# The last 3072 tokens' first product as Strassen's seven block products, in windowed attention with a gated feed-forward on one core

## The chip, the cores and the metric

One core of a Trainium2 chip runs one program. The metric is the device time of a run in microseconds (us). TensorE (PE) multiplies matrices into eight accumulation banks (PSUM); DVE, ACT and POOL are the vector, scalar and general engines; SP only issues DMAs. Each engine executes its own queue in order.

## The reference

```
q, k, v: 8 batches x 8 heads x 576 positions x 64, float32
scores = q @ k.T / sqrt(64); heads 0-3 see the last 32 positions,
         heads 4-7 every fourth position of the last 128
attn   = softmax(scores); x = attn @ v, as 4608 tokens x 512
h = x @ w_in                     # 512 x 2048, the first product
g = h * clip(h + 3, 0, 6) / 6
out = g @ w_out                  # 2048 x 512, the second product
```

## The kernel before

**Precision.** A float32 operand of a large product is split into a high and a low part (`xh`, `xl` for tokens, two rows of `wt[f]` for each weight, `gh`, `gl` for the gated values), and a product is three matmuls: high by high, high by low, low by high.

**Work units.** Tokens come in 12 chunks of 384 (`CH`), the 2048 hidden features in 16 blocks `f` of 128 (`NF`). A step is one pair (chunk, `f`): `gemm1` makes 128 features x 384 tokens with 4 x 3 matmuls of 384 columns into one of the two banks of `ps_h`; `relu`, `gate`, `gate_high`, `gate_low` turn it into `gh` and `gl` on ACT and DVE; two steps later (`LAG`) `gemm2` multiplies three tiles of 128 tokens by the rows of `w_out`, 3 x 3 matmuls of 512 columns, into three banks of `ps_a` that collect over the 16 values of `f`, and at the last one ACT scales them into a tile `o` and stores it.

**Attention.** It is cut into 48 trios of 12 blocks of 32 queries (`trios`, in `_order`). `st_both(ts, tv)` puts the scores of one trio and the values of another on TensorE in one block of 48 small matmuls (`block`), with two banks of `ps_a`; then `normalise` divides the values, `largest` and `shifted` prepare the exponent, `exponent` runs on ACT. `turn_by_blocks` transposes by DVE plus four DMAs on SP's queue. `st_split` writes the finished tokens into `xh` (ACT, `high`) and `xl` (POOL, `low`). `xh` and `xl` hold three chunks at a time.

**Order.** The first 12 trios, the loading and conversion of the weights and the steps of the first two chunks stand in a hand-written order (`ORDER`) that fixes ACT, DVE and SP. After it (`step_at`) TensorE's order is that of the program text, and the other engines' queues are ordered by a planner: among operations that its own estimate of durations has as ready, the one with the lowest `turn_of` value goes first. The remaining trios are placed at half steps by the list `at`, first every 6 halves (3 steps), from the eleventh on every 8. Values of a trio run in the block after its scores.

**SBUF.** Weights, staging tiles, the first trios' loads and `o` share a pool `wpool` of 18 slots of 8 KB a partition.

Of the kernel before, what the change touches and what calls it, by code (L numbers as in the profile page):

```python
# [23 lines left out]
SPARE = 2  # L24
WORK = 12
# [3 lines left out]
NLOAD = 3  # L29
# [4 lines left out]
NEG = -1.0e30  # L34

# [24 lines left out]
h25 Q27 l25 H16 RE26 GL9 w26@H17 k12 k13 k14 v12 v13 v14 M2 RE19 T26 T19 G21 GH26 GH19 Q26 H9 U26 s26 U27 j26 H7  # L60
# [5 lines left out]
def windowed_attention_ffn(ctx: ExitStack, tc: tile.TileContext, qk, vp, w, mask, out):  # L66
# [44 lines left out]
    wpool = ctx.enter_context(tc.tile_pool(name="wpool", bufs=NF + SPARE))  # L111
# [40 lines left out]
    wide = {}  # L152

    def load_tile(t, name, at, n):

        if t >= NWIDE:
            return loads.tile([P, n], F32, name=name, tag=name)
        if t not in wide:
            wide[t] = wpool.tile([P, 4, DM], F32, name="first", tag="w").rearrange("p a n -> p (a n)")
        return wide[t][:, at : at + n]  # L160

    def load_qk(t):
        if t < T and t not in kqs:
            kqs[t] = load_tile(t, "kq", 0, KW + CH)
            ins = nc.sync.dma_start(out=kqs[t], in_=qk[t].rearrange("h d x -> (h d) x"))
            in_turn(ins)
            return ins

    def load_v(t):
        if t < T and t not in vs:  # L170
            v = load_tile(t, "v", KW + CH, TB * W)
            vs[t] = v.rearrange("p (n x) -> p n x", x=W)
            return nc.sync.dma_start(out=v, in_=vp[t].rearrange("h k x -> (h k) x"))
# [67 lines left out]
    def normalise(t):  # L241
        pv = pvs.pop(t)[:, : SLOTS * W].rearrange("p (s x) -> p s x", x=W)
        z = small.tile([P, SLOTS], F32, name="z")
        nc.vector.tensor_scalar_add(z, pv[:, :, D], 1e-9)
# [10 lines left out]
        wide.pop(t, None)  # L255
        if t >= NFIRST:
            load_v(t + NLOAD)
        return ins
# [4 lines left out]
    def block(ts, tv):  # L263

        ps = ps_a.tile([P, 512], F32, name="ps_a") if ts is not None else None
        pv = ps_a.tile([P, 512], F32, name="ps_a") if tv is not None else None
# [17 lines left out]
    def st_both(ts, tv):  # L284
        block(ts, tv)
        if tv is not None:
            normalise(tv)
        if ts is not None:
            largest(ts)
            shifted(ts)  # L290
            exponent(ts)
# [42 lines left out]

    def pieces_of(t):

        b, kind, part = trios[t]
        xu = xfs[t].rearrange("p (u f) -> p u f", u=2)
        half = CH // 2
        to = lambda x: x[:, 2 * kind : 2 * kind + 2, b % 2 * S : b % 2 * S + S]  # L340
        if kind == 0:
            return [(xu, lambda x: to(x)[:, :, half * part : half * (part + 1)])]
        found, at = [], half * part
        while at < half * (part + 1):
            c, i0 = divmod(at, CLS)
            n = min(CLS - i0, half * (part + 1) - at)
            found.append((
                xu[:, :, at - half * part : at - half * part + n],
                lambda x, c=c, i0=i0, n=n: to(x).rearrange("p u (i c) -> p u c i", c=DIL)[:, :, c, i0 : i0 + n],
            ))  # L350
            at += n
        return found

    def high(t):
        b, kind, part = trios[t]
        assert all(read[c] == NF for c in chunks(b - 2, kind, part))
        for src, view in pieces_of(t):
            ins = nc.scalar.copy(view(xh), src)  # L358
        return ins

    def low(t, eng):
        for src, view in pieces_of(t):
            ins = eng.tensor_tensor(out=view(xl), in0=src, in1=view(xh).bitcast(F32), op=ALU.subtract)  # L363
# [4 lines left out]
    def st_split(t):  # L368
        high(t)
        low(t, nc.gpsimd)  # L370
# [9 lines left out]
    steps += [(c, f) for c in range(2, NCH) for f in range(NF)]  # L380
# [6 lines left out]
    wt, staged, converted = {}, {}, set()  # L387
    WN = w.shape[3]

    def load_w(p):  # L390
        st = wpool.tile([P, 4, WN], F32, name="st", tag="w")
        ins = nc.sync.dma_start(
            out=st[:, 0:2].rearrange("p a n -> p (a n)").bitcast(U32), in_=w[p // 2, p % 2].bitcast(U32)
        )
        in_turn(ins)
        staged[p] = st
        return ins

    def parts(p):
        st = staged[p]  # L400
        words = st[:, 0:2].rearrange("p a n -> p (a n)").rearrange("p (n w) -> p n w", w=2)
        return words[:, :, 1], words[:, :, 0], st[:, 2], st[:, 3]

    def cv_product(p):
        if p // 2 not in wt:
            wt[p // 2] = wpool.tile([P, 4, WN], F32R, name="wt", tag="w")
# [24 lines left out]
    def cv_high(p):  # L431
        ins = nc.scalar.copy(wt[p // 2][:, p % 2 * 2], parts(p)[2])
# [3 lines left out]
    def cv_low(p):  # L436
        hi, lo = (wt[p // 2][:, p % 2 * 2 + i] for i in range(2))
# [5 lines left out]

    phs, ts, ghs, gls, po, done = {}, {}, {}, {}, {}, set()
# [4 lines left out]
    def gemm1(n):  # L449
# [5 lines left out]
        for kt in range(NK):  # L455
            a, b = xh[:, kt, r0 : r0 + CH], xl[:, kt, r0 : r0 + CH]
            ks = slice(kt * P, (kt + 1) * P)
            nc.tensor.matmul(ph, lhsT=wt[f][:, 0, ks], rhs=a, start=(kt == 0), stop=False)  # L458
            nc.tensor.matmul(ph, lhsT=wt[f][:, 0, ks], rhs=b, start=False, stop=False)  # L459
            ins = nc.tensor.matmul(ph, lhsT=wt[f][:, 1, ks], rhs=a, start=False, stop=(kt == NK - 1))  # L460
        phs[n] = ph
        return ins
# [15 lines left out]

    def gemm2(n):
        c, f = steps[n]  # L480
        assert 2 * f + 1 in converted
        gh, gl = ghs.pop(n), gls.pop(n)
        first = c not in po
        if first:
            po[c] = [ps_a.tile([P, DM], F32, name="ps_o", tag="ps_a") for _ in range(TT)]
        if f == NF - 1:
            o = wpool.tile([P, TT, DM], F32, name="o", tag="w")
        for tt in range(TT):
            rows = slice(tt * P, (tt + 1) * P)
            nc.tensor.matmul(po[c][tt], lhsT=gh[:, rows], rhs=wt[f][:, 2], start=first, stop=False)  # L490
            nc.tensor.matmul(po[c][tt], lhsT=gh[:, rows], rhs=wt[f][:, 3], start=False, stop=False)  # L491
            ins = nc.tensor.matmul(po[c][tt], lhsT=gl[:, rows], rhs=wt[f][:, 2], start=False, stop=(f == NF - 1))  # L492
            if f == NF - 1:
                if n < len(steps) - 1 or tt < TT - 1:
                    nc.scalar.mul(o[:, tt], po[c][tt], 1.0 / 6.0)
                else:
                    half = DM // 2
                    nc.scalar.mul(o[:, tt, :half], po[c][tt][:, :half], 1.0 / 6.0)
                    nc.vector.tensor_scalar_mul(o[:, tt, half:], po[c][tt][:, half:], 1.0 / 6.0)
                r = c * CH + tt * P  # L500
                nc.scalar.dma_start(out=out[r : r + P, :], in_=o[:, tt])
        done.add(n)
        return ins

# [40 lines left out]
    halves = [(c, f, k) for c in range(2, NCH) for f in range(NF) for k in range(2)]  # L545
# [3 lines left out]
    place(-3, lambda: st_both(NFIRST, None))  # L549
    place(-3, lambda: ats.update({NFIRST: turn_by_blocks(es.pop(NFIRST), "a")}))  # L550
    for i, p in enumerate(at):
        t = NFIRST + i
        more = t + 1 < T
        place(p, lambda t=t, more=more: st_both(t + 1 if more else None, t))
        place(p, lambda t=t: xfs.update({t: turn_by_blocks(xs.pop(t), "xf")}))
        if more:
            place(p, lambda t=t: ats.update({t + 1: turn_by_blocks(es.pop(t + 1), "a")}))
        place(p + 4, lambda t=t: st_split(t))
# [37 lines left out]
    while n < len(steps) + LAG:  # L596
        step_at(n)
        n += 1

# [93 lines left out]
```

## Time and profile before

| | |
|---|---|
| median of 3 runs | 897.35 us (895.88 to 897.6) |
| profiled execution, span | 896.5 us |
| profiled execution, its own time beside the span | not listed; the median run is 0.85 us over the span |
| PE busy | 879.8 us, 98% |
| DVE, ACT, POOL busy | 450.2, 339.4, 43.7 us |
| mean TensorE clock granted | 0.997 |
| moved by DMA | 74.87 MB, mean 84 GB/s |

A row of a group of instructions gives line, engine, operation, tile written <- tiles read, shapes and count, then the busy total in us and the mean of one in ns, then the idle time of the engine just before and what ended it. A row of the timeline gives start, duration, engine and line; in brackets the idle time before it and what ended that. A row of the windows gives the stretch, its length, the busy time of the engines, the granted clock, the DMA share and GB/s. `L458` is a line of the listing above; DMA issues stand under their queue (SPq, ACTq). TensorE's printed durations are pipelined; distances between starts are what one costs.

### The profile page before, as it was taken

The page shows a single profiled execution, that of the slowest core. Times are in us where ns is not written, and L with a number is a line of the kernel's source. Part 1 is how long each engine was busy: PE and PEld are TensorE (multiplying, and loading weights), DVE is VectorE, ACT ScalarE, POOL GpSimd, SP SyncE. Part 2 cuts the span into 40 slices and gives each one's busy share as a digit, 9 for nine tenths or more (in the row PEclk, how much of TensorE's full clock was granted, in tenths as well). Part 3 has the DMA queues.
Part 4 walks back from the last instruction along what each step waited for, and adds up shares of the span by engine and source line. Part 5 has one row for each costly group of instructions (what it writes and reads, how often), then busy time and mean ns, then how long its engine had stood idle before and what let it go on. Part 6 is the DMA issues. An engine that isn't in the chain of part 4 may idle for free.

```text
span 896.5 us, 20572 instructions
## 1 busy us (share of the span) xinstructions
PE 879.8 (98%) x8732; PEld 787.5 (88%) x8732; DVE 450.2 (50%) x952; ACT 339.4 (38%) x661; POOL 43.7 (5%) x60
## 2 busy tenths in 40 slices
PE   7799999999999999999999999999999999999998
PEld 4688898889898899989998999899989998899997
DVE  3899997355545454445444544554454445322222
ACT  3688775333332333223323333233223332422322
POOL 0000000001010100000100010001000100000000
PEclk9999999999999999999999999999999999999999
DMA  8756436132323122113112212222122110100000
GB/s 276 271 152 204 122 114 201 56 95 84 89 87 87 53 88 88 47 48 123 52 47 86 85 51 82 56 81 85 47 64 99 60 28 11 49 1 1 36 1 35
DMA packets 37804, 74.87 MB, mean 84 GB/s; under 512 B 7377, under 2 KB 16593, under 8 KB 37713
## 3 DMA queue, kind: packets, MB, share of 16 engines
q1 hardware_dynamic: 32528, 64.13, 23.3%
q10 hardware_dynamic: 5184, 9.44, 2.8%
q8 instruction: 68, 1.11, 0.5%
q14 instruction: 24, 0.19, 0.1%
HBM read 57.02 MB, written 9.44 MB: 74 GB/s over the span
## 4 chain that ended last, share of the span: by engine, by line
PE 96%; DVE 1%; DMA 1%; ACT 0%; issue 0%; SPq 0%
PE ps_h L458 16%; PE ps_h L459 15%; PE ps_h L460 15%; PE ps_o L490 15%; PE ps_o L492 15%; PE ps_o L491 15%; PE ps_a L211 3%; PE ps_a L193 2%; PE ps_a L296 1%; PE ps_a L203 1%; DMA first<-in_qk 1%; DMA mi<-in_mask 0%; DVE x L247 0%; PE ps_a L270 0%; DVE e L230 0%
## 5 line engine op out<-in xcount | busy, mean ns | idle before, releaser
L458 PE MATMUL ps_h<-xh,wt 128*128 128x384 f32 x768 | 264.0, 344 | 0.0
L460 PE MATMUL ps_h<-xh,wt 128*128 128x384 f32 x768 | 258.6, 337 | 0.0
L459 PE MATMUL ps_h<-xl,wt 128*128 128x384 f32 x768 | 258.6, 337 | 0.0
L469 DVE SCALAR_TENSOR_TENSOR t<-t,ps_h 128x384 f32<-128x384 f32 x192 | 105.0, 547 | 247.9 <-ACT t L466 246.5
L490 PE MATMUL ps_o<-wt,gh 128*128 128x512 f32 x576 | 224.5, 390 | 0.0
L491 PE MATMUL ps_o<-wt,gh 128*128 128x512 f32 x576 | 224.1, 389 | 0.0
L492 PE MATMUL ps_o<-wt,gl 128*128 128x512 f32 x576 | 224.0, 389 | 0.0
L466 ACT ACTIVATE t<-ps_h,three 128x384 f32<-128x384 f32 x192 | 110.7, 577 | 215.7 <-PE ps_h L460 210.4
L477 DVE TENSOR_TENSOR gl<-t,gh 128x384 fp32r<-128x384 f32 x192 | 107.1, 558 | 103.8 <-ACT gh L473 101.4
L458 PEld LDWEIGHTS ps_h<-xh,wt 128*128 128x128 f32 x768 | 144.8, 189 | 8.9
L459 PEld LDWEIGHTS ps_h<-xl,wt 128*128 128x128 f32 x768 | 144.7, 188 | 5.3
L460 PEld LDWEIGHTS ps_h<-xh,wt 128*128 128x128 f32 x768 | 144.6, 188 | 0.0
L473 ACT CAST gh<-t 128x384 fp32r<-128x384 f32 x192 | 98.4, 513 | 110.9 <-DVE t L469 97.3
L492 PEld LDWEIGHTS ps_o<-wt,gl 128*128 128x128 f32 x576 | 108.1, 188 | 22.8
L490 PEld LDWEIGHTS ps_o<-wt,gh 128*128 128x128 f32 x576 | 108.2, 188 | 15.5
L491 PEld LDWEIGHTS ps_o<-wt,gh 128*128 128x128 f32 x576 | 108.2, 188 | 15.5
L363 POOL TENSOR_TENSOR xl<-xf,xh 128x384 fp32r<-128x384 f32 (+3 forms) x54 | 43.1, 808 | 734.9 <-ACT xh L358 734.5
L239 ACT ACTIVATE e<-e 128x384 f32<-128x384 f32 x48 | 25.0, 524 | 139.9 <-DVE e L230 139.8
L211 PEld LDWEIGHTS ps_a<-v,a 64*32 64x32 f32 x1728 | 35.6, 105 | 12.7 <-issue 12.7
L193 PE MATMUL ps_a<-kq 64*32 64x64 f32 x1872 | 45.7, 225 | 0.0
L358 ACT CAST xh<-xf 128x384 fp32r<-128x384 f32 (+3 forms) x72 | 33.6, 532 | 22.7 <-DMA xf<-xf_t 22.6
L211 PE MATMUL ps_a<-v,a 64*32 64x65 f32 x1728 | 41.4, 225 | 0.0
(48 smaller groups left out, 489.3 us busy)
## 6 DMA issues: line engine op xcount, KB each, us to landing
st<-in_w SPq DMA_DIRECT2D x32, 512.0 KB, 4.2
kq<-in_qk SPq DMA_DIRECT2D x39, 416.0 KB, 4.5
v<-in_v SPq DMA_DIRECT2D x39, 390.0 KB, 3.6
out<-o ACTq DMA_DIRECT2D x36, 256.0 KB, 2.3
first<-in_qk SPq DMA_DIRECT2D x9, 416.0 KB, 5.1
first<-in_v SPq DMA_DIRECT2D x9, 390.0 KB, 4.8
a<-a_t SPq DMA_DIRECT2D x144, 24.0 KB, 1.8
xf<-xf_t SPq DMA_DIRECT2D x144, 24.0 KB, 2.5
```

The lines of the kernel that those rows point to most:

```text
L193: return nc.tensor.matmul(ps[at : at + QB, 2 * QB * i : 2 * QB * (i + 1)], lhsT=x[rows, KW + QB * n : KW + QB * (n + 1)], rhs=x[rows, QB * ...
L211: return nc.tensor.matmul(ps[at : at + QB, i * W : (i + 1) * W], lhsT=ats[t][rows, QB * n : QB * (n + 1)], rhs=vs[t][rows, n, :], start=Tr ...
L458: nc.tensor.matmul(ph, lhsT=wt[f][:, 0, ks], rhs=a, start=(kt == 0), stop=False)
L459: nc.tensor.matmul(ph, lhsT=wt[f][:, 0, ks], rhs=b, start=False, stop=False)
L460: ins = nc.tensor.matmul(ph, lhsT=wt[f][:, 1, ks], rhs=a, start=False, stop=(kt == NK - 1))
L466: return nc.scalar.activation(ts[n], phs[n], AF.Relu, bias=three, scale=1.0)
L469: return nc.vector.scalar_tensor_tensor(out=ts[n], in0=ts[n], scalar=6.0, in1=phs.pop(n), op0=ALU.min, op1=ALU.mult)
L473: return nc.scalar.copy(ghs[n], ts[n])
L477: return nc.vector.tensor_tensor(out=gls[n], in0=ts.pop(n), in1=ghs[n].bitcast(F32), op=ALU.subtract)
L490: nc.tensor.matmul(po[c][tt], lhsT=gh[:, rows], rhs=wt[f][:, 2], start=first, stop=False)
L491: nc.tensor.matmul(po[c][tt], lhsT=gh[:, rows], rhs=wt[f][:, 3], start=False, stop=False)
L492: ins = nc.tensor.matmul(po[c][tt], lhsT=gl[:, rows], rhs=wt[f][:, 2], start=False, stop=(f == NF - 1))
```

## The change

Chunks 0 to 3 stay as they were. Chunks 4 to 11 form four groups of two chunks, and the 16 blocks `f` eight pairs. For each group and pair, a 2 x 2 block matrix of tokens (two chunks by two halves of the 512 inputs) times a 2 x 2 block matrix of weights is formed with seven block products (Winograd's form of Strassen's scheme) where four steps of `gemm1` had eight. A block product is two inputs' tiles by three matmuls of 384 columns.

- **Weights.** `combine(k)`, placed at eight half steps of chunks 2 and 3, makes the four weight sums of pair `k` on POOL, splits them on ACT and DVE, and writes them and three plain blocks to a DRAM tile `sums` (11 DMAs on SP's queue). In every group `load_sums` streams `sums` back, 512 KB at a time, into tiles `ring`, eight ahead.
- **Tokens.** Finished tokens of chunks 4 on go by POOL copies into tiles `raw`; `add_tokens` makes four differences on POOL at the last pair of a group, and `fill_cell` splits each of the seven sources into `xh`, `xl` and a seventh pair of tiles after the last use of the old content.
- **A pair.** `pair` orders the seven products over two banks of `ps_h`: products accumulate in `x` and `y`, `kept` copies a bank on ACT, `added` adds a bank on DVE, `gated` is the chain to `gh` and `gl`. The second product's tiles wait in a list `units` and run between the products; a group's six output tiles hold all six banks of `ps_a`.
- **Attention.** Scores of trio t + 2 now share a block with the values of trio t. 17 blocks stand in chunks 2 and 3, about two steps apart; 21 stand in pairs, one in each of the first seven pairs of groups 0 to 2, and use the banks of `ps_h`, `largest` ahead of `normalise`.
- **Slots.** `wpool` has 36 slots of 4 KB; a trio's two loads, a stage and its conversion, and the two weights of an `f` have slots of their own. 16 work tiles (12 before), loads two ahead (three before).

```diff
-SPARE = 2
-WORK = 12
+SLOTS_W = 36
+WORK = 16
-NLOAD = 3
+NLOAD = 2
+PLAIN = 4
+RING = 8
+STEP_US = 4.1
...
+    def combine(k):
+        wa, wb = win[2 * k], win[2 * k + 1]
+        v = w_tile("v", [4, HALF])
+        for i, x in enumerate((wa, wb)):
+            ins = nc.gpsimd.tensor_tensor(
+                out=v[:, 2 * i : 2 * i + 2].rearrange("p a n -> p (a n)"), in0=x[:, 0].bitcast(F32), in1=x[:, 1].bitcast(F32), op=ALU.add
+            )
+            not_before(ins, last_gemm[0])
+        for to, a, b, op in ((3, 2, 3, ALU.add), (2, 0, 2, ALU.subtract), (0, 3, 0, ALU.subtract), (1, 1, 0, ALU.subtract)):
+            nc.gpsimd.tensor_tensor(out=v[:, to], in0=v[:, a], in1=v[:, b], op=op)
+        hi, lo = w_tile("sh", [4, HALF], F32R), w_tile("sl", [4, HALF], F32R)
+        split = nc.scalar.copy(hi, v)
+        nc.vector.tensor_tensor(out=lo, in0=v, in1=hi.bitcast(F32), op=ALU.subtract)
...
+    def load_sums(at):
+        if at < GROUPS * STREAM:
+            ring[at] = w_tile("ring", [2, 2, HALF], F32R)
+            ins = nc.sync.dma_start(out=ring[at].bitcast(F32), in_=sums[at % STREAM])
...
+    def add_tokens(g):
+        (b11, b12), (b21, b22) = ([raws.pop((2 * g + j, k)) for j in range(2)] for k in range(2))
+        t1, t2, t4 = (w_tile("t", [2, CH]) for _ in range(3))
+        minus = lambda to, a, b: nc.gpsimd.tensor_tensor(out=to, in0=a, in1=b, op=ALU.subtract)
+        minus(t1, b12, b11)
+        minus(t2, b22, t1)
+        minus(b12, b22, b12)
+        minus(t4, b21, t2)
+        sources[g] = {A11: b11, A12: b21, S2: t2, S1: t1, S3: b12, A22: t4, S4: b22}
+    def fill_cell(g, i):
+        src = sources[g].pop(i)
+        hi, lo = cell(i)
+        nc.scalar.copy(hi, src)
+        nc.vector.tensor_tensor(out=lo, in0=src, in1=hi.bitcast(F32), op=ALU.subtract)
...
+    def gated(h, g, f, j):
+        x = work_tile("t")
+        nc.scalar.activation(x, h, AF.Relu, bias=three, scale=1.0)
+        nc.vector.scalar_tensor_tensor(out=x, in0=x, scalar=6.0, in1=h, op0=ALU.min, op1=ALU.mult)
+        gh, gl = work_tile("gh", F32R), work_tile("gl", F32R)
+        nc.scalar.copy(gh, x)
+        nc.vector.tensor_tensor(out=gl, in0=x, in1=gh.bitcast(F32), op=ALU.subtract)
+        for tt in range(TT):
+            units.append(lambda tt=tt: unit_part(g, f, j, tt, gh, gl))
+    def multiply(g, k, i, bank, start):
+        at = PRODUCTS * k + i
+        tile_, (h, l) = ring[g * STREAM + at // 2][:, at % 2], cell(i)
+        for kt in range(2):
+            ks = slice(kt * P, (kt + 1) * P)
+            nc.tensor.matmul(bank, lhsT=tile_[:, 0, ks], rhs=h[:, kt], start=(start and kt == 0), stop=False, skip_group_check=True)
+            nc.tensor.matmul(bank, lhsT=tile_[:, 0, ks], rhs=l[:, kt], start=False, stop=False, skip_group_check=True)
+            nc.tensor.matmul(bank, lhsT=tile_[:, 1, ks], rhs=h[:, kt], start=False, stop=(kt == 1), skip_group_check=True)
+        if at % 2:
+            load_sums(g * STREAM + at // 2 + RING)
+        if k == NF // 2 - 1 and g + 1 < GROUPS:
+            fill_cell(g + 1, i)
...
+    def pair(g, k, n, beside):
+        fa, fb = 2 * k, 2 * k + 1
+        bank = lambda: ps_h.tile([P, CH], F32, name="ps_x", tag="ps_h")
+        soon = lambda us: turn_of(n + us / STEP_US)
+        soon(0)
+        x, y = bank(), bank()
+        multiply(g, k, A11, x, True)
+        soon(-8)
+        s = kept(x)
+        soon(1)
+        multiply(g, k, A12, y, True)
+        soon(-8)
+        h = added(s, y)
+        soon(-4)
+        gated(h, g, fa, 0)
+        soon(2)
+        run_units(1)
+        multiply(g, k, S2, x, False)
+        soon(-8)
+        s2 = kept(x)
+        y = bank()
+        soon(4)
+        multiply(g, k, S1, y, True)
+        run_units(2)
+        multiply(g, k, S3, x, False)
+        soon(-8)
+        s = kept(x)
+        h = added(s, y)
+        soon(-4)
+        gated(h, g, fb, 1)
+        soon(7)
+        run_units(3)
+        multiply(g, k, A22, x, False)
+        soon(-4)
+        gated(x, g, fb, 0)
+        soon(10)
+        multiply(g, k, S4, y, False)
+        soon(-8)
+        h = added(s2, y)
+        soon(-4)
+        gated(h, g, fa, 1)
+        soon(11)
+        run_units(3)
+        for step in beside:
+            step()
+        soon(14)
+        run_units(3)
...
-    at = [1, 7, 13, 19, 25, 31, 39, 45, 51, 57]
-    at += [at[-1] + 8 * (i + 1) for i in range(T - NFIRST - 10)]
+    BLOCKS = 16
+    for b in range(BLOCKS + 1):
+        p = round(1 + 4.07 * (b - 1))
+        take(b, lambda step: place(p, step), lambda step: place(min(p + 4, len(halves) - 1), step))
+    for b in range(BLOCKS + 1, T - NFIRST + 2):
+        g, k = divmod(b - BLOCKS - 1, 7)
+        put = lambda step: in_pair.setdefault((g, k), []).append(step)
+        take(b, put, put, ps_h)
+    for k in range(NF // 2):
+        place(4 + 6 * k, lambda k=k: combine(k))
```

More of the change, by code (lines that the diff above doesn't have):

```diff
@@ L289, in st_both @@
             largest(ts)
+        if pool is not None and tv is not None:
+            normalise(tv)
+        if ts is not None:
             shifted(ts)
@@ L477, in gate_low @@
         return nc.vector.tensor_tensor(out=gls[n], in0=ts.pop(n), in1=ghs[n].bitcast(F32), op=ALU.subtract)
-    def gemm2(n):
[L480 to L487, printed above, removed]
-        for tt in range(TT):
[L489 to L501, printed above, removed]
@@ new lines, in store, with out_tile @@
+    def store(o, bank, r, halves=False):
+        if not halves:
+            nc.scalar.mul(o, bank, 1.0 / 6.0)
+        else:
+            half = DM // 2
+            nc.scalar.mul(o[:, :half], bank[:, :half], 1.0 / 6.0)
+            nc.vector.tensor_scalar_mul(o[:, half:], bank[:, half:], 1.0 / 6.0)
+        nc.scalar.dma_start(out=out[r : r + P, :], in_=o)
+    outs = {}
+    def out_tile(c, tt):
+        if (c, tt // 2) not in outs:
+            outs[c, tt // 2] = w_tile("o", [2, DM])
+        return outs[c, tt // 2][:, tt % 2]
@@ new lines, in gemm2_part @@
+    def gemm2_part(n, tt):
+        c, f = steps[n]
+        gh, gl = ghs[n], gls[n]
+        first = f == 0
+        if first and tt == 0:
+            po[c] = [ps_a.tile([P, DM], F32, name="ps_o", tag="ps_a") for _ in range(TT)]
+        rows = slice(tt * P, (tt + 1) * P)
+        nc.tensor.matmul(po[c][tt], lhsT=gh[:, rows], rhs=wt(f, 2), start=first, stop=False)
+        nc.tensor.matmul(po[c][tt], lhsT=gh[:, rows], rhs=wt(f, 3), start=False, stop=False)
+        ins = nc.tensor.matmul(po[c][tt], lhsT=gl[:, rows], rhs=wt(f, 2), start=False, stop=(f == NF - 1))
+        if f == NF - 1:
+            store(out_tile(c, tt), po[c][tt], c * CH + tt * P)
+        return ins
@@ L502, in gemm2, with not_before @@
+    def gemm2(n):
+        assert 2 * steps[n][1] + 1 in converted
+        for tt in range(TT):
+            ins = gemm2_part(n, tt)
+        del ghs[n], gls[n]
         done.add(n)
         return ins
+    HALF = 2 * P
+    PRODUCTS = 7
+    A11, A12, S2, S1, S3, A22, S4 = range(PRODUCTS)
+    GROUPS = (NCH - PLAIN) // 2
+    STREAM = NF // 2 * PRODUCTS // 2
+    sums = tc.dram_tile([STREAM, P, 2, 2, HALF], F32, name="sums")
+    def not_before(ins, name):
+        tc.add_manual_dep(
+            ins.ins, name, mybir.DependencyInfo(mybir.DependencyClass.Sync, mybir.DependencyReason.DATA), reason="not before"
+        )
+        return ins
@@ new lines, in combine @@
+    def combine(k):
[4 more added lines that the diff above has]
+                out=v[:, 2 * i : 2 * i + 2].rearrange("p a n -> p (a n)"), in0=x[:, 0].bitcast(F32), in1=x[:, 1].bitcast(F32), op=ALU.add
+            )
+            not_before(ins, last_gemm[0])
[4 more added lines that the diff above has]
+        nc.vector.tensor_tensor(out=lo, in0=v, in1=hi.bitcast(F32), op=ALU.subtract)
+        for i in range(PRODUCTS):
+            to = sums[(PRODUCTS * k + i) // 2, :, (PRODUCTS * k + i) % 2]
+            if i in (A11, A12, A22):
+                x, at = (wb, HALF) if i == A22 else (wa, i * HALF)
+                not_before(nc.sync.dma_start(out=to, in_=x[:, :, at : at + HALF].bitcast(F32)), split.ins.name)
+            else:
+                row = {S2: 0, S4: 1, S3: 2, S1: 3}[i]
+                nc.sync.dma_start(out=to[:, 0], in_=hi[:, row].bitcast(F32))
+                nc.sync.dma_start(out=to[:, 1], in_=lo[:, row].bitcast(F32))
@@ new lines, in fill_cell, with run_units, unit_part @@
+    def fill_cell(g, i):
[3 more added lines that the diff above has]
+        nc.vector.tensor_tensor(out=lo, in0=src, in1=hi.bitcast(F32), op=ALU.subtract)
+    units = []
+    begun, ended = set(), {}
+    banks = {}
+    def run_units(n):
+        for _ in range(n):
+            units.pop(0)()
+    def unit_part(g, f, j, tt, gh, gl):
+        if g not in banks:
+            banks[g] = [ps_a.tile([P, DM], F32, name="ps_o", tag="ps_a") for _ in range(2 * TT)]
+        at = j * TT + tt
+        bank, first = banks[g][at], (g, at) not in begun
+        begun.add((g, at))
+        ended[g, at] = ended.get((g, at), 0) + 1
+        final = ended[g, at] == NF
+        rows = slice(tt * P, (tt + 1) * P)
+        nc.tensor.matmul(bank, lhsT=gh[:, rows], rhs=wt(f, 2), start=first, stop=False)
+        nc.tensor.matmul(bank, lhsT=gh[:, rows], rhs=wt(f, 3), start=False, stop=False)
+        nc.tensor.matmul(bank, lhsT=gl[:, rows], rhs=wt(f, 2), start=False, stop=final)
+        if final:
+            store(out_tile(PLAIN + g, at), bank, (PLAIN + 2 * g) * CH + at * P, g == GROUPS - 1 and j == 1 and tt == TT - 1)
@@ new lines, in kept, with added @@
+    def kept(bank):
+        s = work_tile("s")
+        nc.scalar.copy(s, bank)
+        return s
+    def added(s, bank):
+        nc.vector.tensor_tensor(out=s, in0=bank, in1=s, op=ALU.add)
+        return s
+    def pair(g, k, n, beside):
[45 more added lines that the diff above has]
+        run_units(3)
@@ L595, in windowed_attention_ffn @@
     assert len(converted) == 2 * NF
-    while n < len(steps) + LAG:
+    while n < len(steps):
         step_at(n)
         n += 1
+    for at in range(len(steps) - LAG, len(steps)):
+        units += [lambda at=at, tt=tt: gemm2_part(at, tt) for tt in range(TT)]
+    turn_of(n - 1)
+    for i in range(A22, PRODUCTS):
+        fill_cell(0, i)
+    for g in range(GROUPS):
+        for k in range(NF // 2):
+            if k == NF // 2 - 1 and g + 1 < GROUPS:
+                turn_of(n - 1)
+                add_tokens(g + 1)
+            pair(g, k, n, in_pair.get((g, k), []))
+            n += PAIR
+    run_units(len(units))
 def _order(batch):
```

155 lines of the change are left out of this document (98 added, 57 removed).

## The prediction

> **What bounds the kernel now.** I read the page first (busy shares, the chain that ended last), then the windows, then what TensorE waited for.
>
> ```profile
> span 896.5 us, 20572 instructions
> PE 879.8 (98%) x8732; PEld 787.5 (88%) x8732; DVE 450.2 (50%) x952; ACT 339.4 (38%) x661; POOL 43.7 (5%) x60
> PE 96%; DVE 1%; DMA 1%; ACT 0%; issue 0%; SPq 0%
> ```
> ```profile
> 0.00:50.00 50.00, 37.84 (x970) 28.73 (x970) 31.47 (x74) 27.12 (x56) 0.59 (x6) 0.97 0.79 266
> 50.00:100.00 50.00, 49.76 (x528) 44.98 (x528) 47.57 (x100) 40.38 (x82) 0.00 (x0) 1.00 0.54 171
> 150.00:200.00 50.00, 50.00 (x471) 44.16 (x470) 23.04 (x46) 17.11 (x32) 1.02 (x1) 1.00 0.31 105
> 450.00:500.00 50.00, 50.00 (x524) 44.91 (x523) 23.77 (x52) 17.00 (x33) 3.39 (x4) 1.00 0.26 79
> ```
> ```profile
> PE ps_a L193 <- issue: 4.1, 2, 3.4
> ```
>
> The chain is 96% TensorE. The windows (length, then PE, PEld, DVE, ACT, POOL busy, granted clock, DMA share, GB/s) show idle TensorE in the first 50 us and none from 150 us on, at clock 1.00. The largest group of TensorE's waits (total, times, longest) is 4.1 us, and by the windows it lies in the start. So in the region of the change a removed matmul is worth its whole start-to-start distance, and a new wait costs in full.
>
> ```profile
> 784.79 0.34 PE L458 MATMUL ps_h<-xh,wt 128*128 128x384 f32 x1
> ...
> 786.87 0.39 PE L490 MATMUL ps_o<-wt,gh 128*128 128x512 f32 x1
> ...
> 788.91 0.34 PE L458 MATMUL ps_h<-xh,wt 128*128 128x384 f32 x1
> ```
> ```profile
> 402.56 0.37 PE ps_h L458
> ...
> 420.39 0.37 PE ps_h L458
> ```
>
> One step is 12 matmuls of 384 columns in 786.87 - 784.79 = 2.08 us (173.3 ns each; the 0.34 us printed is a pipelined duration) and 9 of 512 in 2.04 us (226.7 ns, so 0.68 us for one token tile, three matmuls): 4.12 us. Four steps and one attention block are 420.39 - 402.56 = 17.83 us, so a block of 48 small matmuls costs 17.83 - 16.48 = 1.35 us.
>
> **The change, part by part.** *Matmuls removed.* Tokens 1536 on are 8 of 12 chunks. They are done as 4 groups of two chunks, each 8 pairs of weight blocks: 32 pairs. A pair had 4 steps with 48 first-product matmuls; seven block products of 6 make 42. 32 x 6 = 192 go, x 173.3 ns = **33.3 us**. Second products and attention blocks stay in number. The Trainium skill, page "TensorE: Matmul & The Clock Gate", section "Back-to-back issue gap", gives N / 2.4 + 2.5 ns warm; 162.5 ns each would save 31.2 us. The row differs by 11 ns, and I take the row.
>
> *New handoffs.* A pair is 42 x 0.1733 + 36 x 0.2267 = 15.4 us. Its seven products share the two banks of `ps_h`: ACT copies a bank (`kept`), DVE adds (`added`), and TensorE waits for both before it writes the bank again.
>
> ```profile
> L309 ACT COPY a<-ps_a 128x384 f32<-128x384 f32 x12 | 5.6, 477 | 3.1 <-PE ps_a L296 3.1
> L466 ACT ACTIVATE t<-ps_h,three 128x384 f32<-128x384 f32 x192 | 110.7, 577 | 215.7 <-PE ps_h L460 210.4 <-PE ps_o L491 4.1 <-ACT e L239 0.5
> L473 ACT CAST gh<-t 128x384 fp32r<-128x384 f32 x192 | 98.4, 513 | 110.9 <-DVE t L469 97.3 <-POOL xl L363 8.1 <-DMA xf<-xf_t 3.4
> L469 DVE SCALAR_TENSOR_TENSOR t<-t,ps_h 128x384 f32<-128x384 f32 x192 | 105.0, 547 | 247.9 <-ACT t L466 246.5 <-DMA out<-o 1.3
> L477 DVE TENSOR_TENSOR gl<-t,gh 128x384 fp32r<-128x384 f32 x192 | 107.1, 558 | 103.8 <-ACT gh L473 101.4 <-PE ps_o L491 1.3 <-PE ps_o L492 0.9
> L222 DVE TENSOR_TENSOR e<-ps_a,mi 128x384 f32<-128x384 f32 x36 | 19.8, 549 | 0.6 <-PE ps_a L193 0.6
> ```
> ```profile
> 782.57 0.34 PE L460 MATMUL ps_h<-xh,wt 128*128 128x384 f32 x1
> ...
> 783.01 0.58 ACT L466 ACTIVATE t<-ps_h,three 128x384 f32<-128x384 f32 x1 [0.30 <-PE ps_h L460]
> ```
> ```profile
> 8.38 0.53 ACT e L239
> ...
> 9.05 0.87 PE ps_a L296 x3
> ```
>
> From the last matmul's start to ACT are 0.44 us, that is 0.27 after its slot; ACT to TensorE is 9.05 - 8.91 = 0.14. So `kept` answers in 0.27 + 0.48 + 0.14 = 0.89 us, and `added` in 0.27 + 0.55 + 0.14 = 0.96. What hides the `kept` of A11 is A12 (1.04) and one token tile (0.68), 1.72 us; the same length hides `added` before S1. Spare: 0.83 and 0.76 us, one operation of a busy queue. Later handoffs lie behind two or three tiles and have over 1 us. ACT's work in a pair is 3 x 0.48 + 4 x 0.58 + 4 x 0.51 = 5.8 us, DVE's 3 x 0.55 + 4 x 0.55 + 4 x 0.56 = 6.1 us, of 15.4. I cost the handoffs of a pair without attention at nothing; without that cover each costs its 0.9 us.
>
> *Attention inside pairs.* 17 of the remaining blocks move into chunks 2 and 3, 21 into the pairs, where they take the two `ps_h` banks as well.
>
> ```profile
> 272.41 0.17 DVE L244 TENSOR_SCALAR z<-ps_a 128x6 f32<-128x6 f32 x1 [0.77 <-PE ps_a L193]
> ...
> 275.07 0.56 DVE L230 TENSOR_TENSOR e<-e,mx 128x384 f32<-128x384 f32 x1
> 276.52 0.54 DVE L327 STREAM_TRANSPOSE a<-e 128x384 f32<-128x384 f32 x1
> ```
> ```profile
> 275.66 0.53 ACT L239 ACTIVATE e<-e 128x384 f32<-128x384 f32 x1 [4.61 <-DVE e L230]
> 276.09 0.57 ACT L466 ACTIVATE t<-ps_h,three 128x384 f32<-128x384 f32 x1
> ```
>
> DVE reads the block's banks and shifts for 275.63 - 272.41 = 3.2 us; ACT stood 4.61 us before the exponent although `relu`, queued behind it, was ready by about 274.5 (the block's end, 272.41 - 0.27, then 2.08 us of matmuls and 0.27). Now three tiles (2.04 us) cover the first bank, which the masking add frees after some 0.9 us, and 3.07 us the second, freed before DVE's 3.2 us are over. But the exponent then falls at 3.3 to 3.8 us, where `kept` of A11 is due (2.04 + 1.04 + 0.27 = 3.35), and the transposes (0.54 us this one, and a half-size one) where `added` is due. Bounds: nothing (fits in the 0.76 spare), and 1 us (exponent and transposes both ahead). I take 0.2 us x 21 = **4 us**, nearer the lower end because every unloaded handoff above fits.
>
> *Group changes, three.* In the last pair of a group all seven cells are refilled, 768 columns each: an ACT copy and a DVE subtraction, at most two of the 384-column ones, 7 x 1.03 = 7.2 and 7 x 1.12 = 7.8 us. ACT comes to 13.0 and DVE to 13.9 of 15.4 us, without attention there. POOL prepares four of them:
>
> ```profile
> 338.73 1.02 POOL L363 TENSOR_TENSOR xl<-xf,xh 128x384 fp32r<-128x384 f32 x1 [16.88 <-ACT xh L358]
> ```
> ```profile
> 338.27 0.56 DVE L477 TENSOR_TENSOR gl<-t,gh 128x384 fp32r<-128x384 f32 x1 [0.93 <-ACT gh L473]
> 339.17 0.56 DVE L469 SCALAR_TENSOR_TENSOR t<-t,ps_h 128x384 f32<-128x384 f32 x1 [0.34 <-ACT t L466]
> ```
>
> four of at most 2.04 us, 8 us in a chain, after the last tokens arrive; the cells are due a pair later. A fill that waits in ACT's queue holds `kept` behind it. Bounds 0 and 4 us per change; I take 1.3, as the work still fits: **4 us**.
>
> *Chunks 2 and 3.* Eight `combine` calls (POOL adds, one split on ACT and DVE, 11 writes on SP's queue) and blocks every 9.4 us instead of 13.7. Second products run two steps (8 us) behind their gate, which hides the splits; uncovered they would cost about 2 us each. Scores now run two blocks ahead of their values, so SP may be late by some us.
>
> ```profile
> L330 SPq DMA_DIRECT2D a<-a_t x144: 507/588/1221, 179.8 to 766.4; - x144
> ```
> ```profile
> L501 ACTq DMA_DIRECT2D out<-o x36: 338/339/516, 170.9 to 893.1; - x36
> ```
> ```profile
> st<-in_w SPq DMA_DIRECT2D x32, 512.0 KB, 4.2
> ```
>
> SP's demand: 17 blocks x (8 x 0.59 + 2 x 0.34) = 92, 88 writes x 0.34 = 30 (like the stores, whole partitions to DRAM), 8 ring loads 3: 125 us, in 32 x 4.12 + 17 x 1.35 = 155 us. It fits: 0 (bounds 0 and the rival below). In the pairs SP issues some 9 us in 15.4.
>
> *Stream.* 3.5 x 512 KB per pair is 1.8 MB in 15.4 us, 119 GB/s, below the 171 that ran beside a full TensorE; eight tiles lie ahead (35 us) against 4.2 us to land: 0. Start (slots split, two loads later) and end (same store): 0, bounds +-2 us.
>
> Sum on the profiled execution: 896.5 - 33.3 + 4 + 4 = 871.2 us of span. Only its span is shown; the median of the runs lies 0.85 us above it, so **872 us**.
>
> **Rivals.** (1) *Nothing new waits*: 897.35 - 33.3 = 864. For it: the spares above; against it: ACT's 4.61 us behind a late exponent shows that the planned order isn't the chip's. (2) *The handoffs bind*: exponent, transposes and fills come ahead of `kept` and `added` in most pairs, 0.6 us x 32 = 19 us: 864 + 19 = 883, still faster. For it the 0.76 spare; against it that ACT and DVE are half idle in a pair. (3) *SP's queue becomes the bound of chunks 2 and 3*, and TensorE waits at the blocks for late `a`: if a write of weight sums takes the longest 1.22 us of the row, demand is 92 + 107 + 3 = 202 us, 47 over: 864 + 47 = 911, slower. It decides from (155 + 33 - 95) / 88 = 1.06 us per write; the stores' 0.34 speaks against it, head-of-line waits in one queue for it. (4) *POOL and DVE exclude each other*: a DVE operation with two SBUF inputs waits for a whole POOL one. POOL's 8 us in a group change would push DVE to 13.9 + 8 = 21.9 us, 6.5 over, x 3 = 20 us, 884. In the rows the gate with a PSUM input (339.17) runs inside POOL's 338.73 at its usual 0.56 us, and `gl` with two SBUF inputs ends as POOL starts, so they don't test it. The Trainium skill, page "SBUF — State Buffer", section "Who interferes with whom", states that lock.
>
> **How the numbers follow.** The forecast 0.55 (866 to 880), rival 1 0.08, rival 2 0.22, rival 4 0.05, rival 3 0.10 (0.07 of it slower, 0.03 within 0.2%). A measurement tells about 0.2% from no change. Faster 0.90, same 0.03, slower 0.07. The range 863 to 892 takes in rival 1, rivals 2 and 4 with a few us over, and leaves rival 3 out.
>
> **What would show it.** Right: 384-column matmuls fall from 2304 to 2112 at the same 173 ns; TensorE's waits grow by some 8 us, on ACT `s` copies, DVE adds and group changes; pairs without attention last 15.4 us, those with a block 16.8 to 17. Wrong: waits on `s` in every pair (rival 2), waits for DMA `a` in chunks 2 and 3 (rival 3), DVE operations of over 1 us beside POOL (rival 4), or waits for `ring`.

## The result: 0.6% slower, and the profile after

The changed kernel takes 901.71 us (median; 898.24 to 902.84) against 896.0 us of the kernel before beside it: ratio 1.0061, 95% interval 1.0049 to 1.0074. The forecast was 872 us.

The page of the changed kernel, its span, busy rows and chain:

```profile
span 899.6 us, 20846 instructions
PE 865.2 (96%) x8540; PEld 764.0 (85%) x8540; DVE 552.5 (61%) x1084; ACT 396.5 (44%) x746; POOL 113.2 (13%) x142
PE 83%; DVE 6%; DMA 3%; ACT 3%; SPq 2%; issue 2%; POOL 2%; ACTq 0%; POOLq 0%; DVEq 0%
```

The 192 matmuls are gone (8732 to 8540), but only 83% of the chain is TensorE now, where it was 96%. The windows of the changed kernel (columns as in the prediction) say where:

```profile
150.00:200.00 50.00, 50.00 (x509) 44.32 (x511) 23.00 (x43) 16.69 (x30) 5.68 (x6) 1.00 0.30 97
200.00:250.00 50.00, 45.72 (x610) 40.41 (x598) 28.84 (x59) 14.53 (x30) 21.56 (x28) 0.97 0.54 172
250.00:300.00 50.00, 44.03 (x560) 38.76 (x559) 35.09 (x70) 17.64 (x31) 22.09 (x29) 0.90 0.67 211
300.00:350.00 50.00, 44.74 (x576) 39.56 (x574) 35.95 (x65) 15.00 (x27) 17.30 (x16) 0.97 0.67 219
400.00:450.00 50.00, 50.00 (x521) 44.55 (x520) 28.91 (x63) 18.58 (x36) 2.28 (x5) 1.00 0.40 139
750.00:800.00 50.00, 47.24 (x220) 41.48 (x219) 26.66 (x38) 23.51 (x43) 9.53 (x5) 0.93 0.73 269
```

From 200 to 350 us TensorE is idle for 4.28 + 5.97 + 5.26 = 15.5 us, and the granted clock takes 0.03, 0.10 and 0.03 of 50 us each, up to 8 us more. These are chunks 2 and 3, where weight sums and attention blocks were added. In the pairs it runs full again, but for the third group change (750 to 800 us).

By stages (first matmul of chunk 2, first of the first pair, last one): 176.1, 353.6 and 895.4 us. Chunks 2 and 3 take 177.5 us where the prediction's working has 155; the groups 541.8. At its prices matmuls and blocks are 526.5 there (32 x 15.44, 21 x 1.35, and 4.1 for the last 18 second-product matmuls of chunk 3), and it added 8 for stalls. The start was 4.6 us shorter in this profile (176.1 against 180.7), but between 176 and 181 us in the profiles of the experiments, so I count it as no settled gain.

TensorE's waits in the changed kernel, the two largest, and of the other engines those for the new work (total, times, longest):

```profile
PE ps_h L490 <- DVE t L502: 12.4, 4, 5.2
PE ps_x L670 <- ACT s L680: 3.5, 3, 2.8
ACT xh L382 <- DMA xf<-xf_t: 21.7, 5, 4.7
ACT sh L577 <- POOL v L575: 11.2, 5, 4.4
DVE sl L578 <- ACT sh L577: 8.8, 6, 5.1
```

TensorE waits for the gate of the step before (`t`, DVE), not for the stream, and hardly for the bank copies of the seven products (`s`). The gate is late because ACT and DVE stand in order behind operations that wait: a copy into `xh` for a turned tile (`xf`, a DMA), the split `sh` for POOL's adds, `sl` for `sh`.

**One stall followed.** The longest step (number 29, counted from 0, of the 32 of chunks 2 and 3, 11.1 us instead of 4.1) in the timeline of the changed kernel, queue by queue:

```profile
319.04 1.04 SPq L583 DMA_DIRECT2D sums<-wi  x2
...
324.14 0.45 SPq L587 DMA_DIRECT2D sums<-sl  x1
...
325.69 4.28 SPq L336 DMA_DIRECT2D xf<-xf_t  x4
```
```profile
321.90 0.54 DVE L333 STREAM_TRANSPOSE xf<-x 128x384 f32<-128x384 f32 x1
...
336.42 2.17 DVE L233 TENSOR_TENSOR e<-e,mx 128x384 f32<-128x384 f32 x1
338.51 2.56 DVE L627 TENSOR_TENSOR xl<-t,xh 128x768 fp32r<-128x768 f32 x1
```
```profile
331.33 0.51 POOL L390 COPY raw<-xf 128x384 f32<-128x384 f32 x1 [12.16 <-DMA xf<-xf_t]
331.92 1.84 POOL L616 TENSOR_TENSOR t<-raw 128x768 f32<-128x768 f32 x1
...
335.63 2.54 POOL L616 TENSOR_TENSOR raw<-raw 128x768 f32<-128x768 f32 x1
338.13 2.12 POOL L616 TENSOR_TENSOR t<-raw,t 128x768 f32<-128x768 f32 x1
```
```profile
333.80 0.83 ACT L626 CAST xh<-t 128x768 fp32r<-128x768 f32 x1 [6.23 <-POOL t L616]
```

The attention tile is ready on DVE at 322.4, but SP is issuing writes of weight sums until 324.6; its four turning DMAs go out from 325.69 to 329.97. POOL can copy the tile at 331.33 and only then subtract; ACT stands 6.23 us before the first fill, with the gates behind it. Then DVE's exponent shift takes 2.17 us and a fill 2.56, where 0.56 and 0.95 are usual: they end 0.42 and 0.82 us after the POOL subtractions beside them (338.17, 340.25), as if each had waited for POOL's to be over.

### The profile page after: what moved, and what is told of

Its sections match the earlier page's. It is cut to its first block, busy times and chain, and to the rows that moved or that the text cites. A ratio compares the mean times of both kernels' runs of the same rounds, so it can differ in the third digit from the quotient of the medians.

```text
span 899.6 us, 20846 instructions
## 1 busy us (share of the span) xinstructions
PE 865.2 (96%) x8540; PEld 764.0 (85%) x8540; DVE 552.5 (61%) x1084; ACT 396.5 (44%) x746; POOL 113.2 (13%) x142
## 4 chain that ended last, share of the span: by engine, by line
PE 83%; DVE 6%; DMA 3%; ACT 3%; SPq 2%; issue 2%; POOL 2%; ACTq 0%; POOLq 0%; DVEq 0%
PE ps_o L647 10%; PE ps_o L649 10%; PE ps_o L648 9%; PE ps_x L670 9%; PE ps_x L672 9%; PE ps_x L671 9%; PE ps_h L490 4%; PE ps_h L492 4%; PE ps_h L491 4%; PE ps_o L537 4%; PE ps_o L538 3%; PE ps_o L539 3%; DMA xf<-xf_t 2%; PE ps_b L214 2%; SPq L336 2%
## 5 line engine op out<-in xcount | busy, mean ns | idle before, releaser
L647 PE MATMUL ps_o<-wo,gh 128*128 128x512 f32 x384 | 152.7, 398 | 1.3 <-ACT gh L659 1.3
L649 PE MATMUL ps_o<-wo,gl 128*128 128x512 f32 x384 | 151.3, 394 | 1.4 <-DVE gl L660 1.4
L648 PE MATMUL ps_o<-wo,gh 128*128 128x512 f32 x384 | 150.6, 392 | 0.0
L670 PE MATMUL ps_x<-xh,ring 128*128 128x384 f32 x384 | 131.4, 342 | 2.8 <-ACT s L680 2.8
L671 PE MATMUL ps_x<-xl,ring 128*128 128x384 f32 x384 | 130.2, 339 | 0.0
L672 PE MATMUL ps_x<-xh,ring 128*128 128x384 f32 x384 | 130.1, 339 | 0.0
L490 PE MATMUL ps_h<-xh,wi 128*128 128x384 f32 x256 | 89.8, 351 | 12.4 <-DVE t L502 12.4
L649 PEld LDWEIGHTS ps_o<-wo,gl 128*128 128x128 f32 x384 | 72.4, 189 | 18.4 <-DVE gl L660 2.7
L492 PE MATMUL ps_h<-xh,wi 128*128 128x384 f32 x256 | 87.8, 343 | 0.0
L491 PE MATMUL ps_h<-xl,wi 128*128 128x384 f32 x256 | 87.6, 342 | 0.0
L647 PEld LDWEIGHTS ps_o<-wo,gh 128*128 128x128 f32 x384 | 72.4, 188 | 13.5 <-ACT gh L659 1.8
L648 PEld LDWEIGHTS ps_o<-wo,gh 128*128 128x128 f32 x384 | 72.4, 189 | 10.0
L670 PEld LDWEIGHTS ps_x<-xh,ring 128*128 128x128 f32 x384 | 73.3, 191 | 8.3 <-ACT s L680 3.8
L537 PE MATMUL ps_o<-wo,gh 128*128 128x512 f32 x192 | 77.1, 402 | 0.0
L671 PEld LDWEIGHTS ps_x<-xl,ring 128*128 128x128 f32 x384 | 73.2, 191 | 3.8
```

The lines of the kernel that those rows point to most:

```text
L490: nc.tensor.matmul(ph, lhsT=wt(f, 0)[:, ks], rhs=a, start=(kt == 0), stop=False)
L491: nc.tensor.matmul(ph, lhsT=wt(f, 0)[:, ks], rhs=b, start=False, stop=False)
L492: ins = nc.tensor.matmul(ph, lhsT=wt(f, 1)[:, ks], rhs=a, start=False, stop=(kt == NK - 1))
L537: nc.tensor.matmul(po[c][tt], lhsT=gh[:, rows], rhs=wt(f, 2), start=first, stop=False)
L647: nc.tensor.matmul(bank, lhsT=gh[:, rows], rhs=wt(f, 2), start=first, stop=False)
L648: nc.tensor.matmul(bank, lhsT=gh[:, rows], rhs=wt(f, 3), start=False, stop=False)
```

## The experiments

SP's use below is the sum of its DMA issues in chunks 2 and 3 with the gaps of up to 0.15 us between them closed; stage times are from each kernel's one profile.

**Does the preparation of the weight sums cost it, and which part?**

`e_two_combines`: `for k in range(2): place(4 + 6 * k, ...)` instead of `range(NF // 2)`, the stream reads what is there.

> Leaves out six of the eight weight-sum calls (the stream reads the first two pairs' sums throughout). The stretch from the first matmul of chunk 2 to the first pair is 177.5 us in the changed kernel, its matmuls alone about 154. If the combine work (POOL, ACT, DVE and SP together) is what TensorE waits for, the stretch falls to 160 or less and the run to about 883 us. If the denser attention blocks alone make the stretch slow, at most 5 us go: 896 or more.

`e_two_written`: all eight combines, `for i in range(PRODUCTS if k < 2 else 0)` around the writes; the stream reads what is there.

> All eight combine calls run on POOL, ACT and DVE, but only two of them are written out (22 DMAs on SP's queue instead of 88). Theory SP (the writes hold up the DMAs of xf and a in SP's queue): nearly the gain of leaving the calls out, about 885 to 888 us, and ACT's waits on DMA xf (21.7 us) nearly gone. Theory POOL (the adds and the exclusion of DVE and POOL hold up ACT and DVE): at most 4 us less, 898 or more, with ACT's wait on POOL for the split as before.

Measured 880.94 us (ratio to before 0.9824, 0.9806 to 0.9842) and 886.28 us (0.9888, 0.9857 to 0.9919). Six of eight combines cost 901.7 - 880.9 = 20.8 us, 15.4 of it the writes, 5.4 the sums. Chunks 2 and 3 fall from 177.5 to 154.1 and 160.0 us; the groups stay (542.3, 541.9). Those 154.1 us are the forecast's 155: the blocks, denser than before, cost nothing of their own. With the writes left out and all sums made, TensorE's wait for the gate is down from 12.4 us, in the waits of `e_two_written`:

```profile
PE ps_h L490 <- DVE t L502: 4.7, 2, 2.9
```

**Is it the place of the waiting copies, or the queue that the writes stand in?**

`e_split_late` puts the splits of finished tokens (`st_split`) up to three half steps later, and `high`'s copies behind the latest `gemm1`; `e_writes_act` and `e_writes_pool` change the issuing queue:

```diff
-  not_before(nc.sync.dma_start(out=to, in_=x[...]...), split.ins.name)
+  not_before(nc.scalar.dma_start(...), ...)      # e_writes_act, all 11
+  not_before(nc.gpsimd.dma_start(...), ...)      # e_writes_pool, all 11
```

> The ACT copies into xh in chunks 2 and 3 are held until three half steps later, behind a later first product, so that they don't stand in ACT's queue before their data have landed; nothing is left out. Theory ACT order (relu and gate wait behind a copy that is too early): ACT's waits on DMA xf (21.7 us) go and the run falls by about 10 us to 892. Theory SP capacity (the queue is full anyway): the lateness moves to the values' a or to the POOL copies, at most 3 us less, 899 or more.

> The 88 writes of weight sums are issued from ACT's queue instead of SP's, at some 0.45 us each (5 us of ACT per call). Theory SP: xf and a land earlier and the run falls by 10 to 15 us, to 887 to 892, unless ACT's own queue, now longer, gives half of it back. Theory POOL: no gain or a loss from the longer ACT queue, 900 to 906.

> The 88 writes of weight sums are issued from POOL's queue instead of SP's. Theory SP: xf and a land as early as with the writes left out, and the run falls by 10 us or more, to 887 to 892, if POOL's time to issue them is 1 us each or less (88 us of a queue that has about 100 free in the stretch). If POOL's issue is slower or DVE excludes it, the splits are late and it ends above 905.

Measured 902.87 (1.0064, 1.0042 to 1.0086), 912.8 (1.0185, 1.0161 to 1.021) and 899.56 us (1.0039, 1.0013 to 1.0065). With late copies the wait for `xf` is gone, and the next ones grow, in the waits of that kernel:

```profile
ACT sh L577 <- POOL v L575: 18.8, 6, 6.7
DVE sl L578 <- ACT sh L577: 13.1, 7, 7.2
```

On ACT's queue the writes are in the way of the gates, in the waits of that kernel:

```profile
PE ps_h L490 <- DVE t L502: 18.4, 5, 6.6
```

On POOL's queue SP is relieved (153 to 101 us), but POOL now has adds, copies and issues in one queue: the stretch stays at 179.5 us, 27.5 of it in one step. The other 31 steps take 152.0 us, where they take 167.7 in the changed kernel and 148.6 in `e_two_combines`: relieving SP does take most of the small waits away, and one long one comes in their place, in the waits and on ACT of that kernel:

```profile
PE ps_a L214 <- ACT o L515: 19.2, 1, 19.2
```
```profile
277.40 1.04 ACT L577 CAST sh<-v 128x1024 fp32r<-128x1024 f32 x1 [2.46 <-POOL v L575]
...
284.27 0.83 ACT L626 CAST xh<-raw 128x768 fp32r<-128x768 f32 x1 [5.41 <-POOL raw L390]
291.96 1.04 ACT L577 CAST sh<-v 128x1024 fp32r<-128x1024 f32 x1 [6.86 <-POOL v L575]
292.91 1.08 ACT L515 ACTIVATE o<-ps_o 128x512 f32<-128x512 f32 x2
```

An attention block stands 19.2 us for a bank that `o` frees, and `o` stands on ACT behind two splits and a fill that wait for POOL. `e_writes_act` and `e_writes_pool` landed in neither of their two ranges.

**Fewer writes, adds elsewhere, and both.** `e_five_writes` lays `sums` out so that five DMAs carry the bytes of eleven (the stream then loads four tiles a pair instead of 3.5); `e_adds_dve` has `nc.vector` for `nc.gpsimd` in the adds of `combine` and `add_tokens`; `e_five_dve` has both.

```diff
+  nc.sync.dma_start(out=sums[k, :, 2:6, 0], in_=hi...)   # four blocks at once; lo the same
+  nc.sync.dma_start(out=sums[k, :, 0:2, i], in_=...)     # i = 0, 1; and one for A22
```

> Same sums and bytes, written with 5 DMAs per combine call instead of 11 (the split sums as two DMAs of four rows each, the seven blocks of a pair side by side in DRAM); the stream reads 4 tiles per pair instead of 3.5. Theory SP issue time (40 writes instead of 88 at about 0.45 us): most of what leaving out 66 writes gave (15 us), 48/66 of it, 11 us: about 890 us, the stretch of chunks 2 and 3 at 166. Theory DMA bytes (the writes and the transposes' DMAs share the 16 engines, not the queue): no change, 899 to 903, because the same bytes are written.

> The adds of combine and of the token differences run on DVE instead of POOL (about 3 us of DVE per combine call, 3.8 per group change); the copies into raw stay on POOL. Theory exclusion (DVE operations with two SBUF inputs wait for a whole POOL one, 25 us in the changed kernel's profile): the third group change falls from 20.6 to 18 us, no gl takes over 1 us, and the stretch loses some 5 us: 893 to 896. Theory DVE load (DVE becomes the longer queue in the stretch and at group changes): group changes of 18 us all three, the stretch 3 to 6 us longer, 905 or more.

> Five writes per call and the adds on DVE together. If SP issue and the exclusion are two separate costs, their gains add: 882 to 886. If DVE's load eats the second, as slow as or slower than with five writes alone, 890 to 896.

Measured 901.9 (1.0058, 1.0036 to 1.0079), 900.75 (1.0047, 1.0024 to 1.007), 890.05 us (0.9931, 0.991 to 0.9951). Each alone gives nothing that can be told, both 11.7 us. That fell against my reading up to then, of one bound at a time, and `e_adds_dve` landed in neither of its ranges; 901.9 us is what the rival of `e_five_writes`, the bytes, foretold, which `e_pool_dve` below rules out. `e_five_dve` ends at the edge of its rival's range (890 to 896), but far below five writes alone. By the stages in the table below, both together take 5.6 us from chunks 2 and 3, where five writes alone take 2.0 and the adds alone nothing, and 6.6 us from the groups, where the adds alone take 3.8.

**Bursts or totals; and the two resources apart.** `e_spread` issues the same writes two or three per half step over five half steps, on SP; `e_pool_dve` has the writes on POOL's queue and the adds on DVE; `e_five_late` is `e_five_dve` with `add_tokens(0)` at `last_ - 5` instead of `last_ - 8` and its fills three half steps later; `e_five_pool_late` puts that one's five writes on POOL's queue.

> Edit: the eleven writes of a combine are no longer issued in one burst but in steps of one to three (two inputs' halves, then one or two blocks) over the second to the sixth half step behind it, on the same queue; nothing is left out. In the changed kernel SP issues for 153 us of the 177 us of chunks 2 and 3, gaps of 0.1 us included, in back-to-back runs of up to 48 us; the matmuls there are worth 154. Theory 1 (SP's total issue time is the bound there): spreading changes no total, 898 to 905. Rival (the bursts of 5 us ahead of the attention turns are what hurts): the turns wait for one us instead of five, the long steps go, 884 to 890.

> Edit: the 88 writes on POOL's queue and the combine's and the tokens' adds on VectorE; nothing is left out. Each of the two alone gave nothing (899.6 and 900.8). Theory 1 (two resources are near full in chunks 2 and 3, SP's queue by the writes and POOL by the adds, and one relieved leaves the other): SP falls from 153 to about 101 us, POOL has only copies and issues, the stretch falls from 177 to 158 to 164 us, the third group change to 17.4 us as in the run with the adds on VectorE, 880 to 887. Rival (the bytes written, or their landing, are what hurts, wherever they are issued): the stretch stays over 172, 896 to 903.

> Edit: five writes and adds on VectorE as in the run of 890 us, and the first token sums and the fills of the first seven operands placed three half steps later. There step 29 of chunks 2 and 3 takes 12.35 us, with VectorE waiting 5.0 us in order for a copy of the attention's last output for these tokens. Theory: this wait goes, since the copy is there by then; step 29 falls to 4.3 to 6 and the time to 882 to 886. Rival: the sums and fills then are late for the first pair, which grows by as much as step 29 loses: 888 to 893.

> Edit: the former with its five writes on POOL's queue. Theory (SP's queue is still what delays the turns there): the stretch is 158 to 162 us, 876 to 882. Rival (with five writes SP has slack, so their place is of no account): within 2 us of the former run.

Measured 901.67 (1.005, 1.0031 to 1.0069), 881.99 (0.9837, 0.9806 to 0.9868), 892.45 (0.9948, 0.9929 to 0.9966) and 887.58 us (0.9894, 0.9866 to 0.9923). The last lies between its two ranges.

| kernel | adds on | SP in use, us | chunks 2 and 3 | groups | median |
|---|---|---|---|---|---|
| changed | POOL | 153 | 177.5 | 541.8 | 901.7 |
| e_spread | POOL | 149 | 175.1 | 541.9 | 901.7 |
| e_five_writes | POOL | 136 | 175.5 | 541.7 | 901.9 |
| e_writes_pool | POOL | 101 | 179.5 | 538.0 | 899.6 |
| e_adds_dve | DVE | 149 | 178.1 | 538.0 | 900.8 |
| e_five_dve | DVE | 137 | 171.9 | 535.2 | 890.1 |
| e_five_late | DVE | 138 | 169.4 | 539.5 | 892.5 |
| e_five_pool_late | DVE | 102 | 163.8 | 538.2 | 887.6 |
| e_pool_dve | DVE | 102 | 161.1 | 538.4 | 882.0 |
| e_split_late | POOL | 151 | 174.2 | 540.4 | 902.9 |
| e_writes_act | POOL | 93 | 187.5 | 543.7 | 912.8 |
| e_two_written | POOL | 111 | 160.0 | 541.9 | 886.3 |
| e_two_combines | POOL | 110 | 154.1 | 542.3 | 880.9 |

With the adds on DVE the stretch follows SP's use: 178 at 149 us, 172 and 169 at 137 and 138, 164 and 161 at 102. With them on POOL it hardly moves at 136 (175.5), but falls to 160.0 at 111 where the writes are left out and all sums are made (`e_two_written`), although 23 of DVE's two-input operations are stretched there by 25.5 us in all, as in the changed kernel (25.0). So the writes in SP's queue are the larger cause; the sums cost the 5.4 us beside them, and the adds on POOL undo the gain where the writes move into their queue. Spreading leaves SP's total and gives nothing, so bursts are not the cause. Later fills take step 29's loss away and give it to the first pair (23.1 us there instead of 18.7): the rival of that run was right. TensorE's work in chunks 2 and 3 is worth 154 us; a queue with 153 us to issue in order, whose DMAs wait for other engines in between, can't keep up.

`e_pool_dve` does all the work, and beats both kernels: 14 us below the one before. Its windows and the one wait of TensorE in chunks 2 and 3:

```profile
200.00:250.00 50.00, 46.43 (x674) 40.58 (x673) 36.86 (x80) 16.50 (x32) 23.22 (x40) 0.97 0.59 188
250.00:300.00 50.00, 48.56 (x692) 42.77 (x691) 42.98 (x95) 18.90 (x34) 29.20 (x51) 1.00 0.77 252
300.00:350.00 50.00, 46.44 (x586) 40.93 (x586) 41.80 (x89) 18.37 (x34) 10.86 (x20) 0.97 0.69 233
```
```profile
PE ps_h L490 <- DVE t L502: 5.0, 4, 2.2
```

Idle time falls from 15.5 to 8.6 us, the clock's loss from 8 to 3, though the windows move more bytes a second than in the changed kernel (188, 252 and 233 against 172, 211 and 219 GB/s): bandwidth was not the limit.

## Why the prediction was wrong

- **Matmuls removed: right.** 192 went. The starts of the first matmuls of two pairs in a row, with a block and without, in the changed kernel's timeline:

```profile
442.50 0.34 PE L670 MATMUL ps_x<-xh,ring 128*128 128x384 f32 x1
...
459.36 0.34 PE L670 MATMUL ps_x<-xh,ring 128*128 128x384 f32 x1
...
860.47 0.34 PE L670 MATMUL ps_x<-xh,ring 128*128 128x384 f32 x1
...
876.00 0.34 PE L670 MATMUL ps_x<-xh,ring 128*128 128x384 f32 x1
```

  A pair without attention lasts 15.53 us (forecast 15.4), one with a block 16.86 (16.8 to 17).
- **Handoffs at nothing: right**; rival 2 fell. **Attention in pairs, +4: too much.** 16.86 - 15.53 = 1.33 us is the block's own price of 1.35.
- **Group changes, +4: too little.** The first two cost 1.2 us each, the third 5.1 in its pair (20.6 us) and 1.4 in the next: 8.9. The first pair, which I gave no term, takes 21.5 us instead of 16.9: `kept` stands on ACT behind an exponent whose DVE input waits behind fills. POOL's subtractions are a part of the third change: with them on DVE it is 17.3 to 17.4 us and the pair after 15.5.
- **Chunks 2 and 3 at 0: the step that failed**, 177.5 against 155 us, 22.5 of the 28.4 us between the sum's 871.2 and the measured span of 899.6. "It fits" compared SP's 125 us with 155. First, the terms were small: I took a write as the stores' 0.34 us and no gap between DMAs. The changed kernel's rows:

```profile
L583 SPq DMA_DIRECT2D sums<-wi x24: 377/460/1206, 194.9 to 323.1; - x24
L586 SPq DMA_DIRECT2D sums<-sh x32: 412/466/937, 195.8 to 323.6; - x32
L587 SPq DMA_DIRECT2D sums<-sl x32: 320/449/1802, 196.4 to 324.1; - x32
```

  The medians are 0.45 to 0.47 us, the means 0.49 to 0.57, so 46 us instead of 30, and a gap of 0.04 to 0.1 us stands behind most issues, also behind the turning DMAs, 14 us together: 153 us in all. Second, the test was wrong: rival 3 was given a threshold of 1.06 us per write, from filling TensorE's time and the whole gain, but an in-order queue whose consumers have 8 us of cover is late before it is full: at 137 us of use chunks 2 and 3 still took 172. Rival 3's place and sign were right, its price and threshold not.
- **POOL's adds and exclusion (rival 4): right in kind, priced too high in group changes and left out of chunks 2 and 3.** I gave it 20 us in the three changes, and had no rows that tested it; POOL's subtractions cost TensorE some 4.6 us at the third, exclusion and chain together (20.6 and 16.9 us for the two pairs, with the subtractions on DVE 17.4 and 15.5), and nothing at the first two. In chunks 2 and 3 of the changed kernel, timeline of DVE and of POOL:

```profile
207.59 1.71 DVE L510 TENSOR_TENSOR gl<-t,gh 128x384 fp32r<-128x384 f32 x1 [0.58 <-ACT gh L506]
```
```profile
206.33 2.55 POOL L570 TENSOR_TENSOR v<-wi 128x512 f32<-128x512 f32 x2
```

  `gl`, with two inputs in SBUF, takes 1.71 us instead of 0.56; PSUM-fed operations beside POOL keep their time. From 176 us on 23 two-input operations run over 0.4 us past their line's median, 25.0 us together (13 in chunks 2 and 3, 11.3 us; 10 in group changes, 13.7 us); in the kernel before there is none, in `e_pool_dve` 2 with 0.9 us. The same line in the changed kernel and in `e_pool_dve` (ns, shortest/median/longest):

```profile
L660 DVE TENSOR_TENSOR gl<-t,gh x128: 543/558/2206, 362.0 to 890.2; 128x384 fp32r<-128x384 f32 x128
```
```profile
L660 DVE TENSOR_TENSOR gl<-t,gh x128: 542/558/604, 349.5 to 873.6; 128x384 fp32r<-128x384 f32 x128
```

  The Trainium skill, page "SBUF — State Buffer", section "Who interferes with whom", calls the shared port pair of the two engines an exclusive lock; the 1.71 us that end 0.42 us after POOL's two operations (209.30, 208.88) agree.
- **No term for the clock.** The changed kernel has half-rate windows of 3.4 us, single or in twos, behind idle time of TensorE, 17 us of them in chunks 2 and 3, which cost up to 8 of the 22.5 us lost there. A stall can so be dearer than its length, though not every one is: none follows the 2.2 us of idle time at 232.5 us. The Trainium skill, page "TensorE: Matmul & The Clock Gate", section "What's actually happening", gives a window of 3413 ns; the trace's windows agree.
- **Stream at 0: right.** TensorE never waits for `ring` in a listed wait, with 6.5 us to land against 35 us ahead.

Left open: how much of POOL's part is the exclusion and how much the 5.6 us chain of six adds behind which the splits wait. Moving the adds removes both. Whether another order of POOL's queue would spare `e_writes_pool` its 19.2 us, no run shows. The 5 us of the first pair remain in `e_pool_dve` (22.0 us).

## What to carry to other kernels

Work that is taken off the bounding engine has to be prepared somewhere: price the preparation in the queue in which it stands, with each DMA's issue and gap from rows of the same shape, and compare the queue's use with the cover of its consumers, not with the length of the stage. Where a queue comes near the stage's length, as here, its total counts, and spreading doesn't help. Work that only moves from one late queue to another can show nothing (899.6 us), where leaving it out shows what it costs (15.4 us): leave it out once, and relieve both queues in one run, before calling either harmless.

## What the runs showed of the hardware

The same write costs SP 0.45 us and a gap, and POOL 0.54 to 0.73 us of its own time, in the rows of `e_pool_dve`:

```profile
L583 POOL DMA_DIRECT2D sums<-wi x24: 715/728/839, 196.1 to 308.5; - x24
L587 POOL DMA_DIRECT2D sums<-sl x32: 540/540/549, 202.5 to 311.9; - x32
```

Issuing on POOL did not stretch DVE's two-input operations as POOL's adds did (0.9 against 25.0 us). And four turning DMAs took 4.28 us to issue at 325.69 us, behind a burst of writes, where 2.4 is usual: an issue's own time varies, and what stretched this one no run shows.
